# A fused scan and two-layer kernel: first-block decays spread by TensorE from one load, output halves in tiles of their own, half the warming matmuls

## The chip, the cores and the metric

The kernel runs on one core of a Trainium2 chip. The metric is the device time of one execution in microseconds (us). The time before is the median of three runs. Engines are named as the profile names them: PE is TensorE, DVE is VectorE, ACT is ScalarE, POOL is GpSimd and SP is SyncE, which issues all transfers here.

## What is computed

A gated linear attention (a scan with decays, in chunks) is followed by two fully connected layers over its output:

```python
log_a = np.log(np.clip(a, 1e-06, 1.0))                 # batch 4, heads 8, sequence 768
for c in range(nc):
    cum = np.cumsum(la, axis=-1)
    L = np.exp(cum[:, :, :, None] - cum[:, :, None, :]) * causal
    y_intra = (einsum('bhin,bhjn->bhij', Cc, Bc) * L) @ xc
    y_inter = einsum('bhin,bhnd->bhid', Cc, state) * exp(cum)
    y[:, :, sl] = y_intra + y_inter
    state = decay_full * state + sum_j(B_j x_j * decay_from_j)
x = y.transpose(0, 2, 1, 3).reshape(3072, 256)
h = x @ w_in;   x = np.maximum(0.01 * h, h) @ w_out     # 256 -> 2048 -> 256
h = x @ w_in2;  out = (h * np.cos(h)) @ w_out2
```

The weights arrive as 64-bit numbers and are converted on the chip. Every matrix operand of the two layers is kept as a high and a low part, so that each product of the layers is three matmuls.

## The kernel before, in words

The 768 positions are cut into 6 blocks of 128 positions of each of the 4 batches. A block is 4 attention tiles (t = 4b + j) and then, in each layer, 16 steps f of 128 hidden columns on all 512 tokens. The string JOBS "000110101011" gives the order of the twelve jobs, six blocks in each of two layers; the first three are layer 1 (l = 0) of blocks 0, 1 and 2.

One step of a layer is six matmuls into a sum h (lines 535 to 537), an activation (line 545 in the first layer; lines 548 to 560 in the second), a split into high and low parts (hi, line 277 or 279; lo, line 285 or 287), and six matmuls into the output sum y (lines 573 to 575). y is one PSUM tile of two halves of 512 numbers, made once per job (line 570), in a ring of one. At the end of a job both halves are copied out (line 601 or 626), and those of the second layer are stored (line 629).

An attention tile loads its tokens (line 356), its B and C by heads (line 359) and its decays (line 365, two broadcasts of one row over 64 partitions each). The decays are clipped (line 260), scanned into decay products (line 392) and multiplied with the scores that TensorE makes (mm_cb, line 407; decay, line 414). Then come matmuls into the tile's output (lines 428, 435, 443), the state that is carried on (lines 466, 469), and the copies into x1h and x1l for the first layer (lines 455, 459). Tiles alternate in block 0 between the PSUM tiles "att" and "y"; later blocks use "att" alone. The decay copies of block 0 come straight from the input and each is clipped on GpSimd or VectorE (line 474). For later blocks all decays are loaded once (line 257, tile a48 of 48 rows), clipped on VectorE, stored to a buffer in device memory (line 263), and broadcast from there.

Weights come in 16 pieces per layer (line 311). A piece goes through rebase, low, sign, join, hi and lo (lines 313 to 337), where rebase may run on ScalarE or GpSimd, and join (line 330) on VectorE alone.

The order is planned in advance by the class Order: every operation has a cost on each engine that may run it, a due time (or a slack before the time by which those that read it need it), and the slots of the rings that it takes. The planner goes through time and starts, of all that is ready, what is due first; the outcome is the order in which each engine's queue is written. An engine runs its queue in that order, so an operation that waits holds up all that is behind it on its engine. "Vx" and "Gx" are forms that use the port which VectorE and GpSimd share; where VectorE has such work ready, the planner keeps GpSimd's form back (line 141). Warming matmuls (line 247) of 256 columns, on zeros, keep TensorE busy until the first product of the layers: 22 are put first, then others wherever the plan finds TensorE idle, reckoned at 256 / 2400 us each (line 252).

## Time and profile before

| What | us |
|---|---|
| Median of 3 runs (lowest, highest) | 610.67 (609.89, 612.05) |
| The profiled execution's own time | 613.14 |
| Its span on the core | 611.40 |
| TensorE busy in the span | 595.3 |
| ScalarE, VectorE, GpSimd busy | 358.1, 313.4, 263.5 |

All times inside the profile are counted from the start of the span. Times of matmuls overlap, as they are pipelined: a matmul of 512 columns is shown with 0.39 us, and follows the one before it after 0.23. The clock is the share of full speed that was granted to TensorE: 1.00 is 2.4 GHz and 0.50 is 1.2 GHz, and a number between them is the mean of a stretch that holds both. Busy times of the other engines can be read as they stand.

### The profile page before, as it was taken

What the parts mean: (1) busy time and instruction counts of PE and PEld (TensorE: products, weight loads), DVE (VectorE), ACT (ScalarE), POOL (GpSimd) and SP (SyncE); (2) the same over time, 40 slices, a digit from 0 to 9 for tenths busy, and PEclk for the clock granted to TensorE, in tenths of its full rate; (3) what the DMA queues carried; (4) which work ended last, traced back from release to release, by engine and by line L of the source; (5) the groups of instructions that cost most, each with busy time, mean ns of one, the idle gap of its engine ahead of it and who ended that gap; (6) DMA issues with size and microseconds to landing.
All of it is one profiled execution on the core that took longest, in us unless ns stands there. A gap on an engine that the chain in (4) does not pass through costs nothing.

```text
span 611.4 us, 11576 instructions
## 1 busy us (share of the span) xinstructions
PE 595.3 (97%) x4635; PEld 469.0 (77%) x4635; DVE 313.4 (51%) x577; ACT 358.1 (59%) x572; POOL 263.5 (43%) x232
## 2 busy tenths in 40 slices
PE   7898999999999999999999999999999999999996
PEld 5585787778888887778887778888778788888884
DVE  4699897799005565791005685002555001565664
ACT  1599877978546566455446546445655444755553
POOL 6501005403744465335445435445543543644441
PEclk9799999999999999999999999999999999999999
DMA  8787624863000002321000220100000100000101
GB/s 212 229 271 233 207 72 145 252 192 105 0 1 0 1 0 55 103 88 52 1 0 1 89 86 19 53 0 2 19 2 1 34 1 0 1 1 2 34 1 34
DMA packets 25973, 39.73 MB, mean 65 GB/s; under 512 B 2272, under 2 KB 8416, under 8 KB 25920
## 3 DMA queue, kind: packets, MB, share of 16 engines
q1 hardware_dynamic: 25920, 39.00, 20.9%
q8 instruction: 36, 0.59, 0.4%
q14 instruction: 17, 0.14, 0.1%
HBM read 35.75 MB, written 3.24 MB: 64 GB/s over the span
## 4 chain that ended last, share of the span: by engine, by line
PE 86%; DVE 4%; ACT 3%; DMA 3%; issue 1%; POOL 1%; SPq 1%; DVEq 0%; POOLq 0%; ACTq 0%
PE y L573 14%; PE y L575 13%; PE y L574 13%; PE h L535 13%; PE h L537 13%; PE h L536 13%; PE att L407 2%; PE att L428 2%; PE att L435 2%; DMA x2l<-w_out 1%; PE h L247 1%; POOL abc L260 1%; SPq L365 1%; DMA abc<-abc 1%; ACT k L556 1%
## 5 line engine op out<-in xcount | busy, mean ns | idle before, releaser
L285 POOL TENSOR_TENSOR lo<-u,hi 128x512 fp32r<-128x512 f32 x149 | 192.4, 1293 | 200.9 <-ACT hi L277 68.3
L551 DVE SCALAR_TENSOR_TENSOR k<-k,h 128x512 f32<-128x512 int32 x96 | 65.9, 686 | 181.1 <-ACT k L548 180.9
L545 ACT ACTIVATE u<-h 128x512 f32<-128x512 f32 x96 | 58.1, 608 | 82.5 <-PE h L537 76.4
L277 ACT ACTIVATE hi<-u 128x512 fp32r<-128x512 f32 x136 | 86.0, 634 | 27.2 <-DVE u L560 21.8
L556 ACT ACTIVATE k<-k,half_pi 128x512 f32<-128x512 f32 x96 | 69.6, 725 | 45.7 <-DVE k L551 45.3
L560 DVE TENSOR_TENSOR u<-h,k 128x512 f32<-128x512 f32 x96 | 66.0, 688 | 53.7 <-ACT k L556 52.0
L548 ACT ACTIVATE k<-h 128x512 int32<-128x512 f32 x96 | 57.5, 599 | 49.4 <-PE h L537 49.1
L573 PE MATMUL y<-hi,wo1h 128*128 128x512 f32 x192 | 76.8, 400 | 0.5 <-ACT hi L277 0.4
L573 PE MATMUL y<-hi,wo0h 128*128 128x512 f32 x192 | 76.7, 399 | 0.5 <-DVE u L626 0.2
L535 PE MATMUL h<-x1h,wi0h 128*128 128x512 f32 x192 | 75.5, 393 | 0.0
L575 PE MATMUL y<-lo,wo1h 128*128 128x512 f32 x192 | 75.1, 391 | 0.3 <-DVE lo L287 0.3
L575 PE MATMUL y<-lo,wo0h 128*128 128x512 f32 x192 | 75.1, 391 | 0.0
L574 PE MATMUL y<-hi,wo0l 128*128 128x512 f32 x192 | 75.0, 391 | 0.0
L574 PE MATMUL y<-hi,wo1l 128*128 128x512 f32 x192 | 74.8, 390 | 0.0
L537 PE MATMUL h<-x1h,wi0l 128*128 128x512 f32 x192 | 74.8, 390 | 0.0
L536 PE MATMUL h<-x1l,wi0h 128*128 128x512 f32 x192 | 74.7, 389 | 0.0
L573 PEld LDWEIGHTS y<-hi,wo1h 128*128 128x128 f32 x192 | 36.0, 188 | 11.4 <-DVE x2f L601 1.4
L573 PEld LDWEIGHTS y<-hi,wo0h 128*128 128x128 f32 x192 | 36.1, 188 | 10.8 <-issue 1.9
L575 PEld LDWEIGHTS y<-lo,wo1h 128*128 128x128 f32 x192 | 36.0, 188 | 8.8 <-DVE lo L287 1.1
L575 PEld LDWEIGHTS y<-lo,wo0h 128*128 128x128 f32 x192 | 36.2, 188 | 7.8
L535 PEld LDWEIGHTS h<-x1h,wi0h 128*128 128x128 f32 x192 | 36.0, 188 | 7.9 <-issue 0.2
L537 PEld LDWEIGHTS h<-x1h,wi0l 128*128 128x128 f32 x192 | 36.0, 188 | 7.7
(111 smaller groups left out, 944.2 us busy)
## 6 DMA issues: line engine op xcount, KB each, us to landing
raw<-w_in SPq DMA_DIRECT2D x16, 512.0 KB, 4.2
head<-headp SPq DMA_DIRECT2D x24, 256.0 KB, 3.5
tok<-tokp SPq DMA_DIRECT2D x24, 256.0 KB, 4.1
abc<-a_clip SPq DMA_DIRECT2D x40, 128.0 KB, 4.0
raw<-w_out SPq DMA_DIRECT2D x8, 512.0 KB, 3.7
out_t<-u SPq DMA_DIRECT2D x12, 256.0 KB, 2.7
x2h<-w_out SPq DMA_DIRECT2D x4, 512.0 KB, 4.9
x2l<-w_out SPq DMA_DIRECT2D x4, 512.0 KB, 5.4
```

What stands on the lines that cost most here:

```text
L277: A.activation(out, in_, AF.Copy, scale=scale, bias=bias)
L285: G.tensor_tensor(out=out, in0=a, in1=b, op=op)
L535: PE.matmul(tiles[h], lhsT=wh, rhs=xh[:, c, :], start=(c == 0), stop=False)
L536: PE.matmul(tiles[h], lhsT=wh, rhs=xl[:, c, :], start=False, stop=False)
L537: PE.matmul(tiles[h], lhsT=wl, rhs=xh[:, c, :], start=False, stop=(c == 1))
L545: A.activation(make(u, "u", [128, n], F32), tiles[h], AF.Prelu, alpha=0.01)
L551: V.scalar_tensor_tensor(out=tiles[k].bitcast(F32), in0=tiles[k], scalar=-TWO_PI, in1=tiles[h], op0=ALU.mult, op1=ALU.add)
L556: A.activation(t, t, AF.Sin, bias=half_pi)
L560: V.tensor_tensor(out=t, in0=tiles[h], in1=tiles[k].bitcast(F32), op=ALU.mult)
L573: PE.matmul(o, lhsT=wh, rhs=tiles[g], start=(f == 0), stop=False)
L574: PE.matmul(o, lhsT=wl, rhs=tiles[g], start=False, stop=False)
L575: PE.matmul(o, lhsT=wh, rhs=tiles[r], start=False, stop=(f == KF - 1))
```

## The change

The 48 rows of decays are loaded at the start and clipped on VectorE. Their first 8 rows, those of block 0, are split into a high part (ScalarE) and a low part (VectorE), and for tiles 1 to 3 TensorE spreads two rows over 128 partitions with a 0/1 matrix "pick", in two matmuls of 512 columns into a PSUM tile of the ring "h". The scan reads its decays from there. Tile 0 keeps its two broadcasts. No clip may run on GpSimd any more, nor the scaling of keys (line 397) in block 0, nor the rebase of the first three weight pieces. The identity that the scans add is read from SBUF; its copy in PSUM goes. The output sum y is two tiles, one per half, in a ring of two; in block 0 the PSUM pair of tiles 1 and 3 is two tiles as well, so their decay product and their copies are two instructions each. Warming matmuls after the first 22 are reckoned at 256 / 1200 us, so that half as many fill the same idle time of the plan. Loads are reckoned with a lag of 2.6 instead of 2.3, and tiles of "tok", "head" and "abc" are made in the order of their numbers. The rest of the diff changes how PSUM parts are addressed and the order of two groups of matmuls.

```diff
-STAGGER = 2.0
+STAGGER = 1.0
...
-PSUM_TAGS = {"h": 4, "y": 1}
+PSUM_TAGS = {"h": 4, "y": 2}
 SLOTS = {"x1h": 2, "x1l": 2, "x2h": 1, "x2l": 1, "x2f": 2, "raw": 2, "u": 4, "k": 3, "hi": 3, "lo": 3,
-         "tok": 4, "head": 3, "abc": 4, "st": 12, **PSUM_TAGS}
+         "tok": 4, "head": 4, "abc": 4, "st": 8, **PSUM_TAGS}
...
+                    if any(tag in lines and lines[tag][-1][1] != o["n"] for _, tag in o["make"]):
+                        continue
...
-    od = Order(SLOTS)
+    od = Order(SLOTS, ("tok", "head", "abc"))
...
-    def ident_psum(e):
-        A.activation(make("identp", "h", [128, H, Q], F32), ident, AF.Copy)
-
-    od.add(-97, {"A": 0.55}, ident_psum, reads=["ident"], writes=["identp/x"], make=[("identp", "h")])
+    def const_pick(e):
+
+        o = make("pick", "u", [2 * NB, 2 * NB, Q], F32R)
+        A.activation(o, ident[0:2 * NB, 0, 0:2 * NB].rearrange("p (r i) -> p r i", i=1).to_broadcast([2 * NB, 2 * NB, Q]), AF.Copy)
+
+    od.add(-97, {"A": 0.54}, const_pick, reads=["ident"], writes=["pick"], make=[("pick", "u")])
...
-            od.add(-200 if i < WARM_FIRST else 1e6, {"P": WARM_N / (1200 if i < WARM_FIRST else 2400)}, lambda e, i=i: warm(e, i), reads=["zero"] + (["warm/x"] if i else []),
+            od.add(-200 if i < WARM_FIRST else 1e6, {"P": WARM_N / 1200}, lambda e, i=i: warm(e, i), reads=["zero"] + (["warm/x"] if i else []),
...
+    def split_first(e, p):
+        a = tiles["a48"][0:2 * NB]
+        o = make("a48" + p, "lo", [2 * NB, H, Q], F32R)
+        if p == "h":
+            A.activation(o, a, AF.Copy)
+        else:
+            V.tensor_tensor(out=o, in0=a, in1=tiles["a48h"].bitcast(F32), op=ALU.subtract)
+
-    od.add(None, {"S": 0.5}, load_all, writes=["a48"], make=[("a48", "head")], lag=2.3, slack=8)
+    od.add(-300, {"S": 0.75}, lambda e: None, writes=["begin"])
+    od.add(None, {"S": 0.5}, load_all, writes=["a48"], make=[("a48", "k")], lag=2.6, slack=6)
     od.add(None, {"Vx": 0.335}, lambda e: clip(e, tiles["a48"][:, :, 1:Q]), reads=["a48"], writes=["a48"], slack=6)
-    od.add(None, {"S": 0.5}, store_all, reads=["a48"], writes=["a_clip"], lag=2.3, slack=6)
+    od.add(None, {"A": 0.54}, lambda e: split_first(e, "h"), reads=["a48"], writes=["a48h"], make=[("a48h", "lo")], slack=6)
+    od.add(None, {"Vx": 0.6}, lambda e: split_first(e, "l"), reads=["a48", "a48h"], writes=["a48l"], make=[("a48l", "lo")], slack=6)
+    od.add(None, {"S": 0.5}, store_all, reads=["a48"], writes=["a_clip"], lag=2.6, slack=6)
...
-            od.add(None, {k: COST[k] for k in REB}, rebase, reads=[raw + "/hi"], writes=[w], make=[(w, "k")], slack=slack)
+            od.add(None, {k: COST[k] for k in (REB if l or n > 2 else "A")}, rebase, reads=[raw + "/hi"], writes=[w], make=[(w, "k")], slack=slack)
...
-                SP.dma_start(out=o[Q * s:Q * s + Q, :], in_=(abc if first else a_clip)[r:r + 1, :].to_broadcast([Q, H * Q]))
+                SP.dma_start(out=o[Q * s:Q * s + Q, :], in_=(a_clip if t else abc)[r:r + 1, :].to_broadcast([Q, H * Q]))
...
+        if t == 0 or not first:
+            od.add(None, {"S": 0.95}, load_a, reads=["a_clip"] if t else [], writes=[ab], make=[(ab, "abc")], lag=2.6, slack=slack + 4)
+
+    def banks(t):
+
+        if t < NB and t % 2:
+            return [(tiles["Y"], slice(0, 1)), (tiles["Y2"], slice(1, 2))]
+        return [(tiles["A"], slice(0, 2))]
...
+        def spread_a(e):
+
+            o = make(spread, "h", [128, H, Q], F32) if j < 3 else tiles[spread]
+            for p in "hl":
+                PE.matmul(o, lhsT=tiles["pick"][:, 2 * t:2 * t + 2, :].rearrange("p s i -> p (s i)"),
+                          rhs=tiles["a48" + p], start=(p == "h"), stop=(p == "l"))
+
         def scan(e):
-            f = tiles[ab].rearrange("p h i -> p (h i)")
-            V.tensor_tensor_scan(out=f, data0=f, data1=(tiles["identp"] if first else ident).rearrange("p h i -> p (h i)"),
+            if through:
+                make(ab, "abc", [128, H, Q], F32)
+            f, a = (tiles[k].rearrange("p h i -> p (h i)") for k in (ab, spread if through else ab))
+            V.tensor_tensor_scan(out=f, data0=a, data1=ident.rearrange("p h i -> p (h i)"),
                                  initial=0.0, op0=ALU.mult, op1=ALU.add)
...
-            V.tensor_tensor(out=m, in0=tiles[att][:, :, 0:256], in1=m, op=ALU.mult)
+            m, att_banks = tiles[ab].rearrange("p (g h) i -> p g (h i)", g=2), banks(t)
+            for o, g in att_banks:
+                V.tensor_tensor(out=m[:, g, :], in0=o[:, :, 0:256], in1=m[:, g, :], op=ALU.mult)
...
-        if first:
-            od.add(None, {"Gx": 0.59, "Vx": 0.335}, lambda e: clip(e, tiles[ab][:, :, 1:Q]), reads=[ab], writes=[ab], slack=slack)
...
-        od.add(None, {"Vx": 0.14, "Gx": 0.25}, lambda e: clip(e, tiles[tok][:, 384:512]), reads=[tok + "/p"], writes=[tok + "/p"], slack=slack)
...
-        od.add(None, {"Gx": 0.42, "Vx": 0.2}, bd, reads=[ab, tok + "/b"], writes=[tok + "/b"], slack=slack)
+        if t == 0:
+            od.add(None, {"Vx": 0.335}, lambda e: clip(e, tiles[ab][:, :, 1:Q]), reads=[ab], writes=[ab], slack=slack)
+        if through:
+            od.add(None, {"P": 0.5}, spread_a, reads=["a48h", "a48l", "pick"], writes=[spread], make=[(spread, "h")] if j < 3 else [], slack=slack)
...
+        od.add(None, {"Vx": 0.14}, lambda e: clip(e, tiles[tok][:, 384:512]), reads=[tok + "/p"], writes=[tok + "/p"], slack=slack)
...
+        od.add(None, {"Vx": 0.2} if first else {"Gx": 0.42, "Vx": 0.2}, bd, reads=[ab, tok + "/b"], writes=[tok + "/b"], slack=slack)
...
-                if f == 0 and c == 0:
-                    make(y, "y", [128, 2, n], F32)
-                o = tiles[y][:, c, :]
+                if f == 0:
+                    make(ys[c], "y", [128, n], F32)
+                o = tiles[ys[c]]
...
-                       reads=[g, r, f"wo{l}/{f // 2}h", f"wo{l}/{f // 2}l"] + ([ys[c]] if f else ys[:c]),
-                       writes=[ys[c]], make=[] if f or c else [(y, "y")], by=at + LATE * d)
+                       reads=[g, r, f"wo{l}/{f // 2}h", f"wo{l}/{f // 2}l"] + ([ys[c]] if f else []),
+                       writes=[ys[c]], make=[] if f else [(ys[c], "y")], by=at + LATE * d)
...
-    weights(0, 2.0)
+    weights(0, 0.0)
```

## Rows read from the trace of the kernel before

**Rows 1.** The page: busy us (share of the span) and instructions of each engine

```profile
PE 595.3 (97%) x4635; PEld 469.0 (77%) x4635; DVE 313.4 (51%) x577; ACT 358.1 (59%) x572; POOL 263.5 (43%) x232
```

**Rows 2.** Stages: us, busy of PE, PEld, DVE, ACT, POOL; clock, DMA share, GB/s

```profile
0.00:28.90 28.90, 22.27 (x410) 14.85 (x411) 14.21 (x35) 8.99 (x13) 18.22 (x25) 0.88 0.79 225
...
28.90:51.80 22.90, 22.90 (x123) 18.33 (x126) 22.36 (x45) 22.67 (x37) 1.03 (x1) 1.00 0.81 259
...
51.80:59.00 7.20, 4.39 (x152) 2.72 (x151) 5.91 (x12) 6.20 (x11) 1.87 (x2) 1.00 0.80 263
...
59.00:64.00 5.00, 5.00 (x60) 3.31 (x59) 3.73 (x11) 4.51 (x8) 1.70 (x2) 0.66 0.34 98
...
0.00:80.00 80.00, 70.56 (x974) 50.85 (x975) 60.65 (x128) 55.60 (x86) 23.58 (x31) 0.94 0.75 231
...
100.00:598.00 498.00, 497.18 (x3547) 396.86 (x3547) 228.58 (x404) 284.51 (x458) 233.42 (x196) 1.00 0.13 39
```

**Rows 3.** GpSimd in order of time: start, us, what [idle before it, releaser]

```profile
4.70 1.89 POOL L260 TENSOR_SCALAR abc<-abc 128x504 f32<-128x504 f32 x1 [1.94 <-DMA abc<-abc]
```

**Rows 4.** The chain that ended last, 0 to 70 us: start, us, what

```profile
8.73 1.87 POOL abc L260
...
16.41 1.90 POOL abc L260
...
22.41 3.31 PE h L247 x15
...
39.58 4.18 DMA a_clip<-head
```

**Rows 5.** Stages of the head, columns as in rows 2

```profile
5.00:19.90 14.90, 9.58 (x246) 6.32 (x244) 9.65 (x22) 1.77 (x4) 11.92 (x12) 0.97 1.00 276
...
22.30:25.70 3.40, 3.40 (x31) 2.09 (x26) 0.70 (x3) 3.15 (x5) 2.93 (x4) 0.50 0.86 245
...
25.70:28.90 3.20, 3.12 (x83) 2.42 (x83) 1.22 (x4) 1.27 (x3) 0.32 (x1) 0.96 0.44 125
```

**Rows 6.** Groups of instructions: out<-in, forms, count | busy us, mean ns | idle before

```profile
L392 DVE TENSOR_TENSOR_SCAN abc<-abc,h 128x512 f32<-128x512 f32 x4 | 4.9, 1220 | 7.7 <-POOL abc L260 7.7
...
L287 DVE TENSOR_TENSOR wi0l<-k,wi0h 128x512 fp32r<-128x512 f32 x7 | 4.8, 684 | 0.0
...
L287 DVE TENSOR_TENSOR tok<-tok,abc 128x128 f32<-128x128 f32 x13 | 4.0, 311 | 0.0
...
L260 DVE TENSOR_SCALAR head<-head 48x504 f32<-48x504 f32 x1 | 0.4, 407 | 0.0
...
L277 ACT ACTIVATE k<-raw 128x512 f32<-128x512 f32 x11 | 7.4, 677 | 0.0
```

**Rows 7.** The head, line 330 (weight joins) alone: us, DVE busy (count), clock, DMA share, GB/s

```profile
0.00:28.90 28.90, 1.05 (x2) 0.88 0.79 225
```

**Rows 8.** SyncE's queue in order of time: start, us, what

```profile
13.21 0.34 SPq L359 DMA_DIRECT2D head<-headp  x1
...
22.10 0.71 SPq L257 DMA_DIRECT2D head<-abc  x1
...
43.78 3.66 SPq L365 DMA_DIRECT2D abc<-a_clip  x6
```

**Rows 9.** Waits, 50 to 64 us: us in total, times, longest

```profile
PE att L428 <- DVE abc L414: 2.2, 1, 2.2
...
ACT x2l L277 <- DMA x2l<-w_out: 1.0, 1, 1.0
```

**Rows 10.** TensorE at a change of job: start, us, what [idle before it, releaser]

```profile
477.67 0.47 PE L573 MATMUL y<-hi,wo0h 128*128 128x512 f32 x1 [0.18 <-DVE u L626]
```

**Rows 11.** The chain that ended last, the end of the run

```profile
605.08 0.49 PE y L575
...
606.31 0.60 ACT u L626
...
607.00 0.69 DVE u L626
```

More of the change, by code (lines that the diff above doesn't have):

```diff
@@ L66, with __init__ @@
     GAP = 0.2
-    def __init__(self, slots):
+    def __init__(self, slots, in_line):
         self.slots = slots
+        self.in_line = in_line
         self.ops = []
@@ L114, in run @@
         spare = [o for o in ops if o["spare"]]
+        lines = {}
+        for o in ops:
+            for name, tag in o["make"]:
+                if tag in self.in_line:
+                    lines.setdefault(tag, []).append((int(name[len(tag):]), o["n"]))
+        for line in lines.values():
+            line.sort(reverse=True)
         ready = sorted((o["due"], o["n"]) for o in ops if not left[o["n"]])
@@ L251, in scan_moe_kernel @@
         for i in range(WARM):
[L252 removed]
+            od.add(-200 if i < WARM_FIRST else 1e6, {"P": WARM_N / 1200}, lambda e, i=i: warm(e, i), reads=["zero"] + (["warm/x"] if i else []),
                    writes=["warm/x"], make=[] if i else [("warm", "h")], lag=-Order.GAP, spare=True)
     def load_all(e):
[L257 removed]
+        SP.dma_start(out=make("a48", "k", [2 * NT, H, Q], F32).rearrange("p h i -> p (h i)"), in_=abc)
     def clip(e, a):
@@ L364, in load_a, with bank @@
                 r = 2 * t + s
-                SP.dma_start(out=o[Q * s:Q * s + Q, :], in_=(abc if first else a_clip)[r:r + 1, :].to_broadcast([Q, H * Q]))
+                SP.dma_start(out=o[Q * s:Q * s + Q, :], in_=(a_clip if t else abc)[r:r + 1, :].to_broadcast([Q, H * Q]))
         od.add(None, {"S": 0.83}, load_tok, writes=[tok + k for k in ("/x", "/b", "/p")],
-               make=[(tok, "tok")], lag=2.3, slack=slack + 4)
-        od.add(None, {"S": 0.83}, load_head, writes=[head + "/b", head + "/c"], make=[(head, "head")], lag=2.3, slack=slack + 4)
-        od.add(None, {"S": 0.95}, load_a, reads=[] if first else ["a_clip"], writes=[ab], make=[(ab, "abc")], lag=2.3, slack=slack + 4)
+               make=[(tok, "tok")], lag=2.6, slack=slack + 4)
+        od.add(None, {"S": 0.83}, load_head, writes=[head + "/b", head + "/c"], make=[(head, "head")], lag=2.6, slack=slack + 4)
+        if t == 0 or not first:
[4 more added lines that the diff above has]
+        return [(tiles["A"], slice(0, 2))]
+    def bank(t, g):
+        b = banks(t)
+        return b[g][0][:, 0, :] if len(b) > 1 else b[0][0][:, g, :]
     def attention_tile(b, j, slack):
@@ L375, in attention_tile @@
         tok, head, ab = f"tok{t}", f"head{t}", f"abc{t}"
-        att = "Y" if first and j % 2 else "A"
+        att, spread, through = "Y" if first and j % 2 else "A", f"spread{t % 2}", first and j > 0
         st = [f"st{j}.{2 * b + s}" for s in range(3)]
@@ L381, in scan_tok @@
                 a = tiles[tok][:, 384 + Q * s:384 + Q * s + Q]
-                V.tensor_tensor_scan(out=a, data0=a, data1=(tiles["identp"] if first else ident)[:, 0, :], initial=1.0,
+                V.tensor_tensor_scan(out=a, data0=a, data1=ident[:, 0, :], initial=1.0,
                                      op0=ALU.mult, op1=ALU.bypass)
@@ L400, in mm_cb @@
             if t == 1:
-                make("Y", "y", [128, 2, 512], F32)
-            o, k = tiles["Y" if t < NB and t % 2 else "A"], tiles[f"head{t}"]
+                make("Y", "y", [128, 1, 512], F32)
+                make("Y2", "y", [128, 1, 512], F32)
+            k = tiles[f"head{t}"]
             for r in range(2):
@@ L438, in products @@
         def products(e):
-            k, o = tiles[tok], tiles[att]
+            k = tiles[tok]
             mm_own(0)
-            for s in range(2):
+            for s in (1, 0):
                 for p in range(4):
-                    PE.matmul(o[32 * p:32 * p + 32, s, 384:448], lhsT=k[Q * s:Q * s + Q, 256 + 32 * p:288 + 32 * p],
+                    PE.matmul(bank(t, s)[32 * p:32 * p + 32, 384:448], lhsT=k[Q * s:Q * s + Q, 256 + 32 * p:288 + 32 * p],
                               rhs=k[Q * s:Q * s + Q, 64 * p:64 * p + 64], start=False, stop=True, skip_group_check=True)
@@ L454, in x_hi @@
         def x_hi(e):
-            A.activation(tiles[f"x1h{b}"][:, :, T * j:T * j + T], tiles[att][:, :, 256:384], AF.Copy)
+            for o, g in banks(t):
+                A.activation(tiles[f"x1h{b}"][:, g, T * j:T * j + T], o[:, :, 256:384], AF.Copy)
         def x_lo(e):
             c = slice(T * j, T * j + T)
-            V.tensor_tensor(out=tiles[f"x1l{b}"][:, :, c], in0=tiles[att][:, :, 256:384],
-                            in1=tiles[f"x1h{b}"][:, :, c].bitcast(F32), op=ALU.subtract)
+            for o, g in banks(t):
+                V.tensor_tensor(out=tiles[f"x1l{b}"][:, g, c], in0=o[:, :, 256:384],
+                                in1=tiles[f"x1h{b}"][:, g, c].bitcast(F32), op=ALU.subtract)
         def carry(e, s):
-            new = tiles[att][:, s, 384:448]
+            new = bank(t, s)[:, 384:448]
             o = make(st[s + 1], "st", [128, 2 * D], F32)
@@ L522, in layer @@
         y = f"y{l}.{b}"
-        ys = [f"{y}/{c}" for c in range(2)]
+        ys = [f"{y}.{c}" for c in range(2)]
         on_psum_a, on_sbuf_a, on_v, on_g = 0.06 + 0.42 * sc, 0.1 + 0.42 * sc, 0.07 + 0.54 * sc, 0.1 + 1.13 * sc
@@ L600, in out_f @@
                     t = tiles[xf][:, c, :]
-                    (A.copy if e == "A" else V.tensor_copy)(t, tiles[y][:, c, :])
+                    (A.copy if e == "A" else V.tensor_copy)(t, tiles[ys[c]])
                 od.add(at, {"A": on_psum_a, "V": on_v}, out_f, reads=[ys[c]] + ([f"{xf}/0"] if c else []),
@@ L625, in copy @@
                     t = make(o, "u", [128, n], F32)
-                    (A.copy if e == "A" else V.tensor_copy)(t, tiles[y][:, c, :])
+                    (A.copy if e == "A" else V.tensor_copy)(t, tiles[ys[c]])
                 def store(e, c=c, o=o):
```

23 lines of the change are left out of this document (11 added, 12 removed).

## The prediction

> **What bounds the kernel now.** I began with the busy shares on the page [rows 1]: TensorE is busy 97% of the span and no other engine reaches 60%. So the time is TensorE's stream, and a change can win only where that stream is late, idle or at a low clock. The table by stage shows where [rows 2]. From 100 to 598 us TensorE is idle for 0.8 of 498 us at clock 1.00: nothing of size is to be had there. Three stretches differ. Up to 28.9 us no product of the two layers runs; TensorE is filled with warming matmuls and the attention of block 0. From 51.8 to 59 it is idle for 2.8 us (7.20 less 4.39). From 59 to 64 it is busy, but at a mean clock of 0.66, between the levels 1.2 and 2.4 GHz, right after that idle time: this costs 5 x (1 - 0.66) = 1.7 us. And behind the last product comes a tail of some 5 us.
>
> What sets the head: GpSimd's clips of the decays start when the first load lands, at 4.70 [rows 3], take 1.89 us each, and stand in the chain up to 18.3 [rows 4]. Then the chain goes through fifteen warming matmuls, 3.31 us [rows 4], at half clock, while VectorE is busy for only 0.7 of 3.4 us [rows 5]. VectorE works for 14.2 of the head's 28.9 us [rows 2].
>
> What sets the gap at 51.8: TensorE waits 2.2 us for a decay product on VectorE, and ScalarE, whose work comes before that product, waits 1.0 us for a weight load [rows 9]. That load was late because SyncE issues the load of all decays at 22.10 and can issue the block-1 broadcasts, which stand ahead of weights, only when the clipped copy has been stored: store at 39.58, six issues from 43.78 to 47.44 [rows 4, 8].
>
> **The profiled execution** took 613.14 us (span 611.4), the median of the runs is 610.67, 2.47 less. I work in differences and take them from the median.
>
> **The change part by part.**
>
> *Clips and broadcasts of the first block.* Four GpSimd clips (4 x 1.89 = 7.6 us) go, and six of the first block's eight broadcast issues on SyncE (0.61 each by the row of six, 3.7 us of its queue) [rows 3, 8]. Instead one load of 0.71 us issue moves from 22.10 to the front of SyncE's queue. It lands about one issue after 4.7, at 5.4; clip 0.41, copy on ScalarE 0.68 (nearest row, same row length), remainder on VectorE 0.68 [rows 6], two matmuls at 0.44 (fifteen cold ones of half that width took 3.31 [rows 4]): tile 1's scan can begin near 8.1, where it now follows a clip that ends at 10.6. Queued behind the two matmuls on TensorE are only score products of the same tiles. From there VectorE alone paces the head. Its work there: 14.2 busy now, less 1.1 of weight joins [rows 7], 13.1; plus two clips at 0.41, the remainder 0.68, three key scalings that leave GpSimd at 0.31, and four more instructions from the split tiles, at 0.31 less a quarter of 0.68, 0.14 each [rows 6]: 16.1. The scans read their data from PSUM now; one with its other operand there took 1.22 [rows 6], and I take the same. From 4.7 on without a gap this ends at 20.8, and the last tile adds the 2.0 that VectorE waits now in its steps on TensorE and ScalarE (1.2 busy of 3.2 [rows 5]): the first product not before 22.8. The other end is 27.2: the head as now, with half of the burst gone. VectorE fills 65% of the head's middle now (9.65 of 14.9 [rows 5]) and 98% of the stretch behind the head [rows 2]; midway, 82%, gives 16.1 / 0.82 = 19.6, so 24.3: **-4.6**.
>
> *Fewer warming matmuls.* As far as the burst goes this is in the -4.6. But that burst is what lifted the clock: 0.50 up to 25.7, 0.96 after it [rows 5]. Halve it and the products of the first layer may well start at 1.2 GHz. The price lies between 0 and the 1.7 us of the one such start in the trace, at 59 [rows 2]; I take **+1.7**, because a start after ragged work is just what that row is. The Trainium skill, TensorE: Matmul & The Clock Gate, "Part 1: The HAM clock gate", says that the clock is halved by default and after idling and rises only with sustained activity: by it this edit makes the start cold with near certainty. Without a cold start the total would be 1.7 lower.
>
> *A thinner lead for weights.* In 28.9 to 51.8 VectorE is busy 98%, ScalarE 99% and GpSimd under 5% [rows 2]: weights are converted just in time. Up to 80 us the first two have 60.7 and 55.6 of work [rows 2]. The change adds 2.6 to VectorE (the above, less a clip that it already has) and to ScalarE 0.7 for the copy and 2.0 for three rebases at 0.68 [rows 6] that may no longer go to GpSimd; and TensorE wants it all 4.6 us sooner. That is 122 of 151 engine-us where it was 116 of 160. So some is given back: between 0 and all 4.6. ScalarE has 20 idle us in the head to take work early, VectorE has little; I take **+1.5**, a third.
>
> *Store of the clipped decays early.* The store (landing 4.2 us [rows 4]) moves past weight loads into the head. On SyncE it waits for the clip on VectorE, with token loads behind it; at most that gives back the 3.7 us of issues saved above. The queue now also waits for a head buffer before its load at 13.21 [rows 8], and gets a fourth. The early store frees the block-1 broadcasts and the weights behind them. The gap and its cold stretch are worth 2.8 + 1.7 = 4.5; as VectorE stays nearly full there, I take **-2.5**, of 0 to -4.5.
>
> *Output halves in two tiles.* At a change of job the first product of the new sum waits until both halves are copied, 0.18 at 477.67 [rows 10]. Eleven changes at that make 2.0; some show no wait, so **-1.2**, of 0 to -2.0. At the end the copy of half 0 starts at 606.31, though its last product ended at 605.57, and VectorE's copy runs after ScalarE's, 607.00 to 607.69 [rows 11]. The Trainium skill, PSUM — Partial Sum Buffer, section "PSUM bank collisions raise a hardware error", lets engines touch different banks together, and each half fills a bank of its own: by it nothing in the chip asks for this order. Were the order the chip's after all, the split would bring nothing at the end. I take the wait for one on the tile, which goes. Copy 1 then ends at 607.0 and the second store is issued 0.6 sooner: **-0.6**, of 0 to -0.7.
>
> Stagger, lags and slots change what is due first; behind 100 us the other engines have idle time to hide it: 0.
>
> Sum: -4.6 + 1.7 + 1.5 - 2.5 - 1.2 - 0.6 = -5.7, so 610.67 - 5.7 = **605.0 us**.
>
> **The rivals.**
>
> *All of it lands.* The products start at 22.8 and warm, the lead suffices, the gap goes: -6.1 - 4.0 - 2.0 - 0.6 = -12.7, 598.0. For it: TensorE never waited in 28.9 to 51.8. Against: VectorE's 98% there [rows 2]. Chance 0.2.
>
> *The head is hidden.* Weights are ready no sooner, so what the head gains is waited for before 64 us, and the gap stays: only halves and tail remain, -1.8, 608.9. For it: the two full engines [rows 2]. The case that the one load is issued late, as now, and the scans still wait, ends here as well. Chance 0.16, half on each side of the bound below.
>
> *Slower: starved and cold.* One mechanism, between the first product and 50 us: TensorE starts with one converted piece of weights, runs dry on the next while VectorE still holds attention work, idles, and falls to 1.2 GHz, as at 51.8 to 64, where one such event cost 4.5 [rows 2]. It decides once all 4.6 are given back and one more such event comes beside the -1.8: 610.67 - 1.8 + 4.5 = 613.4. For it: nothing idle to catch up with. Against: ScalarE's idle head, and raw loads that are issued sooner. Chance 0.12.
>
> **How the numbers follow.** The forecast has 0.52. A measurement of this kernel can tell about 0.3%, 1.8 us, from no change. Faster by more: 0.52 + 0.2 + half of 0.16, less 0.02 for the forecast's own slow end: 0.78. Same: the other half and some of that end, 0.10; slower 0.12. The terms at their good ends give 597.4, and the late head of 27.2 with a cold start and a weight wait stays just above no change, 611. The range 597 to 611 leaves out most of the last rival and a little of the first, under 2 in 10.
>
> **What would show it.** Right: no clip on GpSimd; first product at 22.8 to 26; warming matmuls off the chain; a clock under 0.7 in the first 4 us of products; the store of decays issued before 15 us; TensorE idle under 1.5 us between 45 and 64; at the end copy 0 beginning while half 1 still multiplies, and the second store issued 0.6 sooner. Wrong: a first product after 27; new TensorE waits for weights before 50 us; cold stretches in later blocks, where now the clock is 1.00.

## The result, and the profile after

The changed kernel takes **601.09 us** (median of 4 runs, 600.61 to 601.67); the kernel before, timed beside it, 611.14 (4 runs, 609.89 to 612.05). The ratio is 0.984, with a 95% interval of 0.982 to 0.986. The forecast was 605.0 with a range of 597 to 611: the direction and the range held, but the gain forecast, 5.7 us, was little more than half of the 10.0 measured. Two executions far off all others, 966.59 us of the kernel before and 1175.30 of the run a_doublewarm, are left out of the medians and ranges below.

One caution before the traces are compared. The profiled execution of before took 613.14, more than any of its timed runs here, while that of the changed kernel took 600.61, its fastest. The spans differ by 12.6 us where the medians differ by 10.0. The first experiment shows where those 2 us lie.

The page of the changed kernel, where [rows 1] stood at 97%:

```profile
PE 590.3 (99%) x4613; PEld 467.6 (78%) x4613; DVE 313.9 (52%) x586; ACT 356.7 (60%) x572; POOL 262.2 (44%) x228
```

Stages of the changed kernel, with the columns of [rows 2]:

```profile
0.00:24.00 24.00, 21.61 (x405) 13.90 (x405) 16.77 (x47) 11.76 (x20) 5.75 (x12) 0.86 0.76 260
24.00:43.00 19.00, 18.44 (x127) 14.70 (x125) 18.52 (x35) 18.97 (x31) 3.78 (x3) 1.00 0.99 281
43.00:50.00 7.00, 6.33 (x87) 4.49 (x93) 6.58 (x16) 6.96 (x11) 1.31 (x2) 1.00 0.85 256
50.00:64.00 14.00, 14.00 (x243) 10.03 (x244) 12.29 (x29) 12.95 (x21) 2.58 (x3) 1.00 0.68 192
100.00:585.00 485.00, 485.00 (x3418) 389.90 (x3417) 228.28 (x403) 271.33 (x438) 230.50 (x194) 1.00 0.12 36
```

The first product starts at 24.05 (28.95 before). The clock stays at 1.00 from there on: the stretch at 0.66 of [rows 2] has no counterpart, and of the 2.8 us of idle time at 51.8 only 0.67 is left at 43, with 0.56 behind the very first product. From 100 to 585 us TensorE has no idle time at all. In the list of waits of TensorE these two are all that is left before 64 us inside the stream of products (the line with x1l and the one with L518; the other falls into the head); [rows 9] answers to it:

```profile
PE att L482 <- DVE st L515: 0.7, 1, 0.7
PE att L482 <- DVE st L518: 0.7, 1, 0.7
PE h L586 <- DVE x1l L508: 0.6, 1, 0.6
```

In the head, VectorE's scans (order of time: start, duration). Those of tiles 1 to 3 now read a PSUM tile and still take 1.2 us; the last starts at 14.16, where it stood at 18.36:

```profile
5.46 1.21 DVE L437 TENSOR_TENSOR_SCAN abc<-abc,ident 128x512 f32<-128x512 f32 x1
...
8.16 1.21 DVE L437 TENSOR_TENSOR_SCAN abc<-h,ident 128x512 f32<-128x512 f32 x1
...
14.16 1.22 DVE L437 TENSOR_TENSOR_SCAN abc<-h,ident 128x512 f32<-128x512 f32 x1
```

GpSimd's clips are gone. What sets the chain from 16 us up to the first product is now ScalarE, which converts weights (lines 302 and 350) between the copies of the tiles (line 503); [rows 4] answers to it. The first line is the stretch from 16 to 24 us with the columns of [rows 2]: ScalarE is busy for all 8.00 us of it, VectorE for 6.68. The others are of the chain:

```profile
16.00:24.00 8.00, 7.04 (x172) 4.61 (x171) 6.68 (x23) 8.00 (x14) 2.94 (x3) 0.89 0.60 197
...
16.28 1.24 ACT raw L350
...
19.09 1.24 ACT raw L350
...
22.30 0.47 ACT x1h L503
...
23.32 0.52 ACT wi0h L302
23.84 0.33 ACT x1h L503 x2
```

SyncE's queue: the store of the decays is issued at 9.00, and the block-1 broadcasts no longer wait for it (24.70; [rows 8] had 43.78):

```profile
9.00 0.35 SPq L277 DMA_DIRECT2D a_clip<-k  x1
...
24.70 2.51 SPq L390 DMA_DIRECT2D abc<-a_clip  x4
27.38 0.46 SPq L336 DMA_DIRECT2D raw<-w_in  x1
```

And the end, in order of time. The copy of half 0 starts while half 1 is still multiplied, and VectorE's copy follows the last product at once ([rows 11]):

```profile
593.88 0.59 ACT L676 COPY u<-y 128x512 f32<-128x512 f32 x1 [1.31 <-PE y L625]
...
594.15 0.39 PE L625 MATMUL y<-lo,wo1h 128*128 128x512 f32 x1
594.50 1.40 SPq L679 DMA_DIRECT2D out_t<-u  x2
594.64 0.69 DVE L676 COPY u<-y 128x512 f32<-128x512 f32 x1 [1.35 <-PE y L625]
```

**Where the time went, by the two traces.** I count every one of the 2,304 products at 0.2267 us, their usual distance (0.68 for three), and call *lost* what passes beyond that from the start of one product to the start of the next thing on TensorE. The lines of the table, rounded, add up to the spans' difference.

| Part of the span, us | before | changed | difference |
|---|---|---|---|
| up to the first product | 28.95 | 24.05 | -4.9 |
| lost between products, up to 90 us | 5.8 | 3.6 | -2.3 |
| matmuls of attention behind the first product | 36.6 | 35.3 | -1.3 |
| lost from 90 us to 15 us ahead of the last product | 10.9 | 7.6 | -3.3 |
| lost in the last 15 us | 1.5 | 1.5 | 0 |
| behind the start of the last product | 5.5 | 4.7 | -0.8 |

Of the third line, 0.7 us is the stretch at half clock of [rows 2] once more: one group of attention matmuls of block 1, at 60.9, takes 1.84 us where the others of its kind take 1.14. The other 0.6 is no gain. It is the first score matmuls of block 1, which the kernel before runs at 36.0 and the changed one at 21.5, ahead of its first product.

Of the 3.3 us behind 90 us, some 2.7 lie at the changes of job. In the kernel before, at seven of the eleven changes, the first product of a new sum starts 0.43 to 0.57 us behind the product ahead of it, where 0.23 is usual, and the one behind it follows 0.31 to 0.34 later. In the changed kernel the first product starts after 0.23 at all eleven. One change, before and then after:

```profile
327.64 0.39 PE L537 MATMUL h<-x2h,wi1l 128*128 128x512 f32 x1
328.07 0.50 PE L573 MATMUL y<-hi,wo1h 128*128 128x512 f32 x1
...
318.04 0.39 PE L587 MATMUL h<-x2h,wi1l 128*128 128x512 f32 x1
318.27 0.39 PE L623 MATMUL y<-hi,wo1h 128*128 128x512 f32 x1
```

### The profile page after: what moved, and what is told of

Same layout as the page of the kernel before. It is cut to its first block, busy times and chain, and to the rows that moved or that the text cites. A ratio compares the mean times of both kernels' runs of the same rounds, so it can differ in the third digit from the quotient of the medians.

```text
span 598.8 us, 11526 instructions
## 1 busy us (share of the span) xinstructions
PE 590.3 (99%) x4613; PEld 467.6 (78%) x4613; DVE 313.9 (52%) x586; ACT 356.7 (60%) x572; POOL 262.2 (44%) x228
## 4 chain that ended last, share of the span: by engine, by line
PE 92%; ACT 3%; DVE 3%; DMA 1%; issue 1%; SPq 0%; DVEq 0%; ACTq 0%
PE y L623 15%; PE h L585 14%; PE y L625 14%; PE y L624 14%; PE h L587 14%; PE h L586 14%; PE att L453 2%; PE att L475 2%; PE att L482 2%; DMA x2h<-w_out 1%; DMA head<-headp 1%; ACT k L606 0%; DVE u L610 0%; DVE k L601 0%; DVE k L355 0%
## 5 line engine op out<-in xcount | busy, mean ns | idle before, releaser
L310 POOL TENSOR_TENSOR lo<-u,hi 128x512 fp32r<-128x512 f32 x156 | 202.4, 1299 | 213.9 <-PE y L625 70.6
L302 ACT ACTIVATE hi<-u 128x512 fp32r<-128x512 f32 x131 | 82.6, 631 | 20.0 <-DVE u L610 14.2
L586 PEld LDWEIGHTS h<-x1l,wi0h 128*128 128x128 f32 x192 | 36.1, 188 | 8.2 <-DVE x1l L508 0.9
```

Of the source, the lines that this page charges most:

```text
L302: A.activation(out, in_, AF.Copy, scale=scale, bias=bias)
L310: G.tensor_tensor(out=out, in0=a, in1=b, op=op)
L586: PE.matmul(tiles[h], lhsT=wh, rhs=xl[:, c, :], start=False, stop=False)
```

## Experiments

Kernels whose name begins with b are made from the kernel before, those with a from the changed one. "Planned anew" says that the planner ran on the edit, so that other instructions moved too; "same order" says that every queue is otherwise as it was. The table has the medians and ratios (to the kernel before on the same chip, with 95% interval) first; then one trace each, read as in the table above ("lost after" goes from 90 us to 15 us ahead of the last product).

| Run | median, us | ratio | first product | lost to 90 us | lost after | attention | end |
|---|---|---|---|---|---|---|---|
| b_again | 609.87 | 0.9985 (0.9966 to 1.0005) | 25.73 | 7.45 | 10.6 | 37.0 | 5.5 |
| b_halfburst | 609.90 | 0.9981 (0.9963 to 1.0000) | 25.49 | 6.7 | 10.5 | 35.9 | 5.5 |
| b_earlystore | 609.58 | 0.9988 (0.9964 to 1.0012) | 25.94 | 5.2 | 10.5 | 35.9 | 5.5 |
| b_clipdve | 608.97 | 0.9964 (0.9945 to 0.9982) | 26.92 | 3.3 | 11.2 | 35.9 | 5.5 |
| a_again | 601.41 | 0.9838 (0.9818 to 0.9859) | 24.97 | 3.6 | 7.6 | 35.3 | 4.7 |
| a_doublewarm | 602.18 | 0.9851 (0.9827 to 0.9875) | 27.95 | 2.2 | 7.6 | 35.3 | 4.7 |
| a_onewarm | 602.14 | 0.9850 (0.9827 to 0.9873) | 24.87 | 3.9 | 7.6 | 35.3 | 4.7 |
| a_ywhole | 607.76 | 0.9938 (0.9918 to 0.9959) | 27.14 | 3.6 | 11.6 | 35.3 | 5.4 |
| a_bcast | 606.75 | 0.9938 (0.9912 to 0.9964) | 25.54 | 5.6 | 8.6 | 36.4 | 4.8 |
| a_oldplan | 604.01 | 0.9889 (0.9859 to 0.9918) | 25.19 | 4.0 | 10.2 | 35.3 | 4.7 |
| a_rebgx | 601.73 | 0.9851 (0.9821 to 0.9880) | 24.55 | 3.6 | 7.6 | 35.3 | 4.7 |
| a_latestore | 603.59 | 0.9881 (0.9852 to 0.9909) | 24.99 | 6.0 | 7.6 | 35.3 | 4.7 |

**The kernel before, once more (b_again).** No edit but a blank line.

> The kernel before once more, unchanged. Its profiled execution was 2.0 us above the median of its timed runs, and the spans of the two profiles differ by 12.6 us where the medians differ by 10.05. Theory: the stretch at half clock behind the idle time at 52 to 59 us (1.7 us) is not there in every execution, so this profile shows a time of 610 to 613 with that stretch, or 608.5 to 611 without it. Rival: the gap itself changes in length between executions, with the clock fall always behind it.

The theory did not hold: the stretch at half clock was there again. The rival held as far as it went, for the gap was longer. But what differed most, by 3.2 us, was the head, which neither named. TensorE in order of time: the same burst of fifteen warming matmuls, the first product, the gap (idle time and what ended it in brackets), and a product at half clock behind it:

```profile
20.82 1.81 PE L248 MATMUL h<-hi 128*128 128x256 bf16 x15
...
25.73 0.47 PE L536 MATMUL h<-x1h,wi0h 128*128 128x512 f32 x1
...
55.75 0.47 PE L429 MATMUL att<-abc,tok 64*32 64x64 f32 x16 [3.11 <-DVE abc L415]
...
57.77 0.63 PE L538 MATMUL h<-x1h,wi0l 128*128 128x512 f32 x1
```

In the first profile the burst took 3.38 us at a clock of 0.50 [rows 5], here 1.81 at 1.00 (the distance of two of these matmuls halves from 0.22 to 0.11). That changed from one execution to another of the same program. So the kernel before starts its products 3 us sooner in one execution than in another; yet the total moved by 1.55 only (613.14 to 611.59), for the decay product of block 1 then makes TensorE wait 3.11 us instead of 2.16, and the clock falls earlier. The head of the kernel before was in part hidden by this gap: my second rival, true of the kernel before. The times of all its executions range from 608.5 to 615.0, those of the changed kernel from 600.6 to 602.1.

**Half the burst, same order (b_halfburst).**

```diff
     def warm(e, i):
+        if i >= WARM_FIRST and i % 2:
+            return
         PE.matmul(tiles["warm"][:, 0:WARM_N], lhsT=tiles["zero"][:, 0:128], rhs=tiles["zero"][:, 0:WARM_N], start=True, stop=True)
```

> The kernel before with the same order of everything on every engine, but every second warming matmul after the first 22 left out. Theory of the prediction: the burst of fifteen was on the path at half clock; with seven or eight left the products start 1.5 to 1.9 us sooner (27.0 to 27.5), but at half clock, which gives back up to 1.7: time 609 to 611. If the clock is up all the same, as in the changed kernel, 609 to 609.5. Rival, the burst is not what the products wait for: start at 28.9 as before, 611.

609.90, beside 609.87 for the same kernel with all of them: by themselves fewer warming matmuls give nothing that can be measured in the kernel before. In the trace the burst is seven matmuls, at half clock as in the first profile:

```profile
21.17 1.68 PE L249 MATMUL h<-hi 128*128 128x256 bf16 x7
```

It takes 1.7 us less than the fifteen did there. The products start at 25.49, at full speed (0.23 apart from 26.2 on), and 2.6 us of waits for decay products between 48 and 57 take back what the start gave.

**The store of the decays early, same order (b_earlystore).** The load is issued behind tile 0's loads, the clip behind tile 0's scan, the store behind the first weight load; the 48 rows get a buffer of their own ("x2f").

```diff
-        for o in od.run():
+        todo = od.run()
+        load, fix, save = (next(o for o in todo if o["n"] == n) for n in early)
+        todo = [o for o in todo if o["n"] not in early]
...
+        put(load, lambda p: "tok0/x" in p["writes"])
+        put(fix, lambda p: p["writes"] == ["abc0"] and p["engine"] == "V")
+        put(save, lambda p: "raw0.0/lo" in p["writes"])
+        for o in todo:
```

> The kernel before with the load of all decays issued behind tile 0's loads, its clip behind tile 0's scan and its store behind the first weight load; the order is otherwise kept, and the 48 rows lie in a buffer of their own. Theory: the late store made SyncE late with the block-1 broadcasts and weights; the idle time at 52 to 59 us shrinks from 2.8 to under 1 and the clock stays up: 606.5 to 608. Rival, VectorE and ScalarE are full there and the store does not matter: the gap stays at 2.5 us or more, 610 to 611.5.

Undecided in the kernel before: 609.58 with an interval that holds 1. In its trace the gap is in two pieces, 0.92 and 0.87, and the clock stays up, but that gain of 2 us is within what executions of this kernel differ by. The reverse was tried in the changed kernel (a_latestore, below).

**No clip on GpSimd (b_clipdve), planned anew.**

```diff
-            od.add(None, {"Gx": 0.59, "Vx": 0.335}, lambda e: clip(e, tiles[ab][:, :, 1:Q]), reads=[ab], writes=[ab], slack=slack)
+            od.add(None, {"Vx": 0.335}, lambda e: clip(e, tiles[ab][:, :, 1:Q]), reads=[ab], writes=[ab], slack=slack)
...
-        od.add(None, {"Gx": 0.42, "Vx": 0.2}, bd, reads=[ab, tok + "/b"], writes=[tok + "/b"], slack=slack)
+        od.add(None, {"Vx": 0.2} if first else {"Gx": 0.42, "Vx": 0.2}, bd, reads=[ab, tok + "/b"], writes=[tok + "/b"], slack=slack)
```

(the same for the clip of tok, which gets {"Vx": 0.14})

> The kernel before, planned anew with no clip on GpSimd and the scaling of keys of block 0 on VectorE; the eight broadcasts by transfers stay. Theory, GpSimd's clips set the head: the first product comes 2 to 4 us sooner, 607 to 609.5. Rival, the broadcasts and the loads behind them set it (SyncE's queue and the landings): the fourth pair still lands near 16.4, the scan of tile 3 starts at 16.8 to 17.5 instead of 18.4, and the first product comes at most 1.5 us sooner: 609.5 to 611.

608.97: 0.9 us below b_again and, by the ratio, 1.1 to 3.4 below the kernel before, and steadier (607.9 to 609.6). VectorE's scans in order of time:

```profile
4.85 1.22 DVE L392 TENSOR_TENSOR_SCAN abc<-abc,h 128x512 f32<-128x512 f32 x1
...
16.48 1.21 DVE L392 TENSOR_TENSOR_SCAN abc<-abc,h 128x512 f32<-128x512 f32 x1
```

The fourth scan moved from 18.36 to 16.48 only, but not for the rival's reason: its clip runs at 15.54, and VectorE waits for no decay load there. The chain up to the first product goes through a weight load and ScalarE's work behind it instead:

```profile
9.08 7.08 DMA raw<-w_in
...
16.77 0.37 ACT x1h L455
```

The first product, at 26.92, is no sooner than in b_again. What this run has over b_again lies between the products: lost time up to 90 us fell from 7.45 to 3.3. Whether the clips alone do that is not shown, for the new plan also issues the load of all decays at 16.12 (22.10 before) and the block-1 broadcasts at 39.08 (43.78 before).

**The changed kernel with each late warming matmul issued twice (a_doublewarm), same order.** The base for all of the following is a_again, the changed kernel itself, at 601.41 and 0.9838. The last four runs, from a_bcast on, were made on another chip; by the ratios, each to the kernel before on its own chip, they differ from a_again by 6.1, 3.1, 0.8 and 2.6 us, where the medians say 5.3, 2.6, 0.3 and 2.2.

> The changed kernel once more, to stand beside the next three on the same chip: 600.5 to 602.

```diff
     def warm(e, i):
+        if i >= WARM_FIRST:
+            PE.matmul(tiles["warm"][:, 0:WARM_N], lhsT=tiles["zero"][:, 0:128], rhs=tiles["zero"][:, 0:WARM_N], start=True, stop=True)
```

> The changed kernel with the same order, but each warming matmul after the first 22 issued twice, about as many as the old reckoning fills in. Theory, fewer warming matmuls is a gain because those at half clock stand in front of ready work: 1 to 2.5 us slower than the changed kernel, 602 to 603.5, with the first product at 25 to 26.5. Rival, TensorE is waiting anyway while they run, so that they are hidden: 600.5 to 601.5, first product at 24.0 to 24.6.

602.18, 0.8 us more, which the intervals do not tell from none. The first product comes 3 us later than in a_again, at 27.95, but then nothing has to wait: both waits before 50 us are gone and 1.4 us of lost time with them. The time is at the low end of the theory, though the first product is later than it said; in the trace half of the later start is made good.

**One warming matmul in all (a_onewarm), same order.**

```diff
     def warm(e, i):
+        if i:
+            return
```

> The changed kernel with the same order and a single warming matmul in all. The term +1.7 of the prediction is priced here: TensorE is at 1.2 GHz when the products of the first layer begin, 1.5 to 2 us are lost behind that, and the matmuls of block 0 run slow as well, up to 1 us more: 602.5 to 604. Rival, the attention of block 0 alone brings the clock up, or the slow matmuls are hidden behind VectorE: 600.5 to 601.8.

602.14, 0.7 more than a_again and between the two ranges; the executions overlap (601.7 to 602.6 beside 601.0 to 602.1). Here the start is cold: products in order of time, 0.42 to 0.43 apart up to 28.0, then 0.23:

```profile
26.73 0.63 PE L587 MATMUL h<-x1h,wi0h 128*128 128x512 f32 x1
27.16 0.63 PE L588 MATMUL h<-x1l,wi0h 128*128 128x512 f32 x1
27.59 0.63 PE L589 MATMUL h<-x1h,wi0l 128*128 128x512 f32 x1
...
28.64 0.40 PE L589 MATMUL h<-x1h,wi0l 128*128 128x512 f32 x1
28.87 0.39 PE L587 MATMUL h<-x1h,wi0h 128*128 128x512 f32 x1
```

Six products lose 0.2 each, 1.2 us, and the waits at 25 and 44 us that the changed kernel has at that point are gone in return. So a cold start costs some 0.7 net, hardly clear of noise, and all the warming together is worth no more.

**The output sum as one tile again (a_ywhole), planned anew.** The ring has one place, and block 0's two parts become views of one such tile.

```diff
-                if f == 0:
-                    make(ys[c], "y", [128, n], F32)
-                o = tiles[ys[c]]
+                if f == 0 and c == 0:
+                    make(y, "yy", [128, 2, n], F32)
+                o = tiles[y][:, c, :]
```

> The changed kernel, planned anew with the output sum as one tile of two halves in a ring of one, as before; block 0 keeps its two parts, as views of one tile. Theory: the waits at changes of job come back (about 0.3 us at each of eight, 2.3) and the tail is 0.6 to 0.9 longer: 3 us slower, 603.5 to 604.5. Rival, the plan finds other work for TensorE at those places: only the tail is longer, 601.5 to 602.3.

607.76, 6.3 us slower: twice the theory. Of the profile's 6.9 us, 2.2 lie ahead of the first product, 4.0 behind 90 us and 0.7 at the end. Behind 90 us the changes of job are back: the first product of the new sum is late at seven of eleven, by 0.92 us at one and by 0.20 to 0.34 at six. TensorE's waits hold two of the seven by name, the largest and one of 0.18 for VectorE's copy (line 676); the timeline shows the largest:

```profile
139.12 0.39 PE L587 MATMUL h<-x1h,wi0l 128*128 128x512 f32 x1
...
139.64 0.57 ACT L651 COPY x2f<-yy 128x512 f32<-128x512 f32 x1
...
140.27 0.50 PE L623 MATMUL yy<-hi,wo0h 128*128 128x512 f32 x1 [0.76 <-ACT x2f L651]
```

The product at 140.27 waits 0.76 us for ScalarE's copy of the second half, which ended at 140.21.

The 2.2 us ahead of the first product can't be put down to block 0's shared tile alone. In this execution TensorE's clock was at half just there (columns of [rows 2]), and the last nine warming matmuls took 2.10 us in front of the products; in the two profiles of the changed kernel the clock was at 1.00 by then:

```profile
24.60:28.00 3.40, 3.40 (x44) 2.52 (x44) 3.40 (x7) 2.58 (x6) 0.95 (x1) 0.50 0.76 218
```

**Block 0's decays by eight broadcasts, clipped on VectorE (a_bcast), planned anew.** The spread by TensorE, its split and "pick" go; load, clip and store of all decays stay early, by a due time of -90.

```diff
-                SP.dma_start(out=o[Q * s:Q * s + Q, :], in_=(a_clip if t else abc)[r:r + 1, :].to_broadcast([Q, H * Q]))
+                SP.dma_start(out=o[Q * s:Q * s + Q, :], in_=(abc if first else a_clip)[r:r + 1, :].to_broadcast([Q, H * Q]))
...
-        att, spread, through = "Y" if first and j % 2 else "A", f"spread{t % 2}", first and j > 0
+        att, spread, through = "Y" if first and j % 2 else "A", f"spread{t % 2}", False
...
-        if t == 0:
+        if first:
```

> The changed kernel, planned anew, with block 0's decays by eight broadcasts and a clip on VectorE for each tile, as the kernel with no clip on GpSimd had them; the one load, its clip and its store stay early and the spread by TensorE goes. Theory, the spread is worth something of its own because six broadcasts put later loads back: scan of tile 3 at 16.5 to 17.5 instead of 14.2, first product 1.5 to 3 us later than the 24.0 to 25.0 of the changed kernel; as a later start is partly made good before 60 us, 602.0 to 603.5. Rival, the conversion of the first weights on ScalarE sets the first product, and the spread is hidden: 601 to 601.8.

606.75, 5.3 us slower: both were too low. The scans of tiles 2 and 3:

```profile
13.10 1.21 DVE L434 TENSOR_TENSOR_SCAN abc<-abc,ident 128x512 f32<-128x512 f32 x1
...
18.08 1.22 DVE L434 TENSOR_TENSOR_SCAN abc<-abc,ident 128x512 f32<-128x512 f32 x1
```

The last scan comes 4 us later than the changed kernel's, but the first product only 0.6 to 1.5 later (25.54 against 24.97 and 24.05). The rest is lost further on, save 0.6 us of attention, which is block 1's first score matmuls behind the first product again. TensorE's waits, of which the second line is in the head:

```profile
PE att L479 <- DVE st L515: 3.0, 3, 1.3
...
PE y L472 <- DVE abc L458: 0.7, 1, 0.7
PE att L472 <- DVE abc L458: 0.6, 1, 0.6
```

The three of 3.0 us in total stand at 46, 63 and 122 us, the one of 0.6 at 66. That VectorE went into the products with less weight work behind it would explain them; the trace shows the waits, not this cause.

**Stagger, lags and slack as before (a_oldplan), planned anew.**

```diff
-STAGGER = 1.0
+STAGGER = 2.0
...
-    od.add(None, {"S": 0.5}, load_all, writes=["a48"], make=[("a48", "k")], lag=2.6, slack=6)
+    od.add(None, {"S": 0.5}, load_all, writes=["a48"], make=[("a48", "k")], lag=2.3, slack=6)
...
-    weights(0, 0.0)
+    weights(0, 2.0)
```

(the lag in the same way in all six loads and stores)

> The changed kernel, planned anew with the stagger of 2.0, the lags of 2.3 and the slack of 2.0 for the first layer's weights, as before. The prediction put these at 0: 600.5 to 602.3. Rival, the stagger is what took the waits for VectorE out of 40 to 60 us: they come back, idle time of 2 us or more there, 603 to 605.

604.01, 2.6 more, which I had put at 0. The three numbers together matter, as the rival has it for the stagger, but the place is another. The wait that returns is one line of TensorE's list:

```profile
PE att L482 <- DVE st L518: 2.6, 4, 0.7
```

Four waits of 0.5 to 0.7 each for a carried state, at 42, 119, 260 and 357 us: three of them in later blocks, where the engines have idle time by the shares and the one instruction that counts is still late. Which of the three numbers does it was not separated.

**Rebase on GpSimd allowed (a_rebgx), planned anew.**

```diff
-            od.add(None, {k: COST[k] for k in (REB if l or n > 2 else "A")}, rebase, reads=[raw + "/hi"], writes=[w], make=[(w, "k")], slack=slack)
+            od.add(None, {k: COST[k] for k in REB}, rebase, reads=[raw + "/hi"], writes=[w], make=[(w, "k")], slack=slack)
```

> The changed kernel, planned anew, with the rebases of the first three weight pieces allowed on GpSimd again. In the changed kernel ScalarE is busy without a gap from 16 to 25 us and stands in the chain up to the first product, while GpSimd has little to do. Theory, ScalarE now sets the head: two or three rebases of 0.57 us leave it, first product 0.5 to 1.5 us sooner, 600.0 to 601.2. Rival, VectorE sets it and GpSimd's rebases hold its port: no gain or a loss, 601.2 to 602.5.

601.73 beside 601.41: no difference clear of noise. First product 24.55, between the two of the changed kernel. ScalarE stands in the chain there, but taking three rebases off it (GpSimd runs them at 13.20, 15.16 and 18.20) does not bring the products forward.

**The store of the decays late (a_latestore), same order.** The 48 rows get a buffer of their own ("x2f").

```diff
-        for o in od.run():
+        todo = od.run()
+        save = next(o for o in todo if o["writes"] == ["a_clip"])
+        todo.remove(save)
+        todo.insert(next(i for i, o in enumerate(todo) if o["reads"] == ["a_clip"]), save)
+        for o in todo:
```

> The changed kernel with the same order, but the store of the clipped decays put just ahead of the first broadcast that reads it on SyncE's queue (near 24 us instead of 9), with the 48 rows in a buffer of their own. SyncE then waits about 4 us for the landing with weight loads behind. Theory, the early store is worth the gap that it removed: idle time of TensorE in 40 to 60 us grows by 1 to 3 us, 602.5 to 604.5. Rival, as the kernel before with an early store suggests, the store decides little and VectorE's and ScalarE's order decides the gap: 601 to 602.

603.59, 2.2 more: the theory. SyncE's queue holds the broadcasts back for the store (issued at 24.85), and the weight load behind them is issued at 32.44, where the changed kernel issues it at 27.38:

```profile
29.97 2.38 SPq L390 DMA_DIRECT2D abc<-a_clip  x4
32.44 0.53 SPq L336 DMA_DIRECT2D raw<-w_in  x1
```

The chain to TensorE's wait goes through this load. TensorE in order of time: the wait, and products at half clock behind it:

```profile
46.10 0.34 PE L482 MATMUL att<-head,st 32*32 32x64 f32 x16 [1.86 <-DVE st L518]
...
48.56 0.63 PE L624 MATMUL y<-hi,wo0l 128*128 128x512 f32 x1
...
51.93 0.40 PE L624 MATMUL y<-hi,wo0l 128*128 128x512 f32 x1
```

1.86 us of idle time for a carried state, and seven products that take 0.2 longer each. It is the gap of the kernel before in small, with its clock fall, brought back by one moved transfer.

## Why the prediction was right, and where its terms were off

- **Head, -4.6.** Measured -4.9 in the traces (28.95 to 24.05) and 24.97 in a second execution. The size came out, the mechanism only in part, so that 24.3 for 24.05 is partly luck. VectorE's busy time up to 24 us is 16.77, of it 2.00 in three weight joins: 14.8 for the 16.1 reckoned without joins. But VectorE does not pace the head alone, as the prediction has it: from 16 us on it is ScalarE that is busy without a gap. Taking the clips from GpSimd is not enough (b_clipdve, last scan at 16.48, first product no sooner); with the spread by TensorE the last scan starts at 14.16, and with broadcasts in its place at 18.08 (a_bcast). And the start of the kernel before was no fixed number, but 25.7 or 28.9 by the clock under the burst.
- **Cold start, +1.7.** Did not happen: the products start at 1.00. The step that failed is "Halve it and the products of the first layer may well start at 1.2 GHz". Its premise, that the burst is what lifted the clock, was read from one execution: in b_again the whole burst already runs at 1.00. Ahead of the first product the changed kernel has 63 warming matmuls for 91, and 342 others for 320. TensorE was busy for 4.99 us of 10 to 15 us, at a mean clock of 0.59, before the clock rose (columns of [rows 2]):

```profile
10.00:15.00 5.00, 4.99 (x125) 3.04 (x128) 3.84 (x11) 0.95 (x2) 0.72 (x1) 0.59 1.05 381
```

  b_halfburst, with 57 warming matmuls, starts at full speed too, but a_ywhole, with 61, starts at half: their number alone does not settle it. Where the start is made cold (a_onewarm) it costs some 0.7 net. The Trainium skill, TensorE: Matmul & The Clock Gate, "Part 1: The HAM clock gate", has the clock rise only with sustained activity. That agrees with a_onewarm, whose first products stand 0.43 apart; my step from "fewer warming matmuls" to "cold" did not hold.
- **Thinner lead, +1.5.** Measured 0.56 + 0.67 = 1.2 us of new waits. The size is about right, but by luck: the term is for weights, and neither wait is for one. Both are for VectorE's attention work, the part x1l of block 0's last tile and a carried state. That an earlier start is in part given back was seen in both kernels: 3.2 us of head gave 1.55 in b_again, and 3 us cost 0.8 to 1.6 in a_doublewarm. Between the two profiled executions of the changed kernel, though, 0.92 of head made 0.95 of time.
- **Gap and cold stretch, -2.5.** Undersized: the 2.8 + 1.7 of before fell to the 0.67 counted above under the lead. The early store is 2.2 of it by a_latestore, so that term alone was fair in the changed kernel, though in the kernel before an early store by itself brought nothing clear. The rest may go with the clips' move (b_clipdve, 3.3 lost up to 90 us for 7.45), which was not tried apart from the plan that came with it.
- **Halves, -1.2 and -0.6.** The largest miss. The end gave 0.8, the changes of job some 2.7; putting the tile back costs 6.3 in all; of the 6.9 of its profile 4.7 lie behind 90 us and at the end. I read one wait of 0.18 [rows 10] as the price of a change; what the undoing showed is 0.2 to 0.9 each at seven of eleven, with a second product 0.1 late behind it, and the list of waits names only some of them. The order of the copies at the end was indeed the tile's and not the chip's: ScalarE's copy at 593.88 now runs beside the product at 594.15, each in its own bank. The Trainium skill, PSUM — Partial Sum Buffer, section "PSUM bank collisions raise a hardware error", lets engines touch different banks together, and this trace agrees.
- **Stagger and lags, 0.** Wrong: 2.6 by a_oldplan, most of it in later blocks that I had passed over because their engines are half idle.
- **Rivals.** "All of it lands" came nearest, 598.0 for 601.1 (its 4.0 for the gap is 0.5 less than the 2.8 + 1.7 of that term). "Starved and cold" did not occur in the changed kernel; the 1.86 us of idle time and the clock fall of a_latestore are such an event in small, though TensorE waits there for a carried state.

The parts that were undone one by one cost 6.3, 5.3, 2.6, 2.2 and 0.8 us, 17 in all, for a change that brought 10. They don't add; as I read it, each removes a wait behind which another stands. Parts put into the kernel before by themselves (burst, store, clips) brought 0 to 2. Some parts were not undone by themselves: the sizes of the rings "head" and "st", the order of tiles by number, the scaling of keys, the place of the identity, and block 0's pair of tiles. A sum of terms was the wrong form for this; what the terms lacked was that the later wait is only reached when the earlier one is gone.

## What to carry to other kernels

Where every engine's queue is written in advance, price an edit by where the next wait in line stands, not by the time of the instruction it removes: in the kernel before, a start 3.2 us earlier was worth half of itself, for a later gap absorbed the rest. A PSUM tile of two banks can hold up everything that wants either half; splitting it took no more PSUM, and undoing the split cost 4.0 us behind 90 us, most of it at the changes of job. And profile a kernel twice before reckoning with a stretch that hangs on TensorE's clock: here two executions of one program differed by 3.2 us at the first product and by 1.55 at the end.

## What the runs showed of the hardware that was not expected

- The same fifteen warming matmuls took 3.38 us in one execution and 1.81 in another, with TensorE at 1.2 or 2.4 GHz, though all that came before them was the same program.
- In a_onewarm the products came 0.43 us apart from 26.7 to 28.0 us, half speed, in a stretch for which the clock column reads 1.00. The distance of two products is the safer sign of the level.
- A scan that reads its data from PSUM took 1.19 to 1.22 us, as from SBUF.
